# A rule by lag for what stands behind each burst of attention scores, in a two-layer-pair prompt kernel on one core

## The chip, the core and the metric

The kernel runs on one core of one Trainium2 chip. The metric is the device time of one execution in microseconds (us), and the number that counts is the median of several runs. A profile of one execution is shown beside it. In what follows PE is the matrix engine (with its weight loads listed as PEld), ACT the scalar engine, DVE the vector engine, POOL the GpSimd engine, and SP the engine that issues most DMAs.

## What is computed

```python
B, S, D, H = 1, 2048, 576, 32            # Dh = D // H = 18
def _A_ref(x, wq, wk, wv, wo):           # 32 query heads, one shared key and value head
    q = (x @ wq) as (B, H, S, Dh);  k = x @ wk;  v = x @ wv
    scores = einsum("bhqd,bkd->bhqk", q, k) * Dh ** -0.5
    return concat_heads(softmax(scores) @ v) @ wo
def _B_ref(x, wqkv, w_phi, wo):          # linear attention with a learned feature map
    phi(t) = concat(softmax(t @ w_phi), softmax(-t @ w_phi))        # per head
    kv = phi(k).T @ v;  z = phi(k).sum(tokens)
    return (phi(q) @ kv / (phi(q) @ z + 1e-6)) @ wo
x = x + _A_ref(layernorm(x));  x = x + _B_ref(layernorm(x))
x = x + _A_ref(layernorm(x));  x = x + _B_ref(layernorm(x))
```

The two pairs of layers are called layer 0 and layer 1 below.

## The kernel before

Tokens are worked on in 16 tiles of 128. The exact attention of a layer (`attend`) is one long loop over 32 groups: a tile of 128 query tokens with half of the heads makes a group, and a group has 16 key tiles. For one key tile there are two **units** of scores. A unit (`expose`) is two matmuls of 56 rows by 512 columns (line 595) into a score buffer `sc` of two PSUM banks, and one exponential on ACT (line 1101, 128x1024) into a tile `pt` in SBUF. There are three `sc` buffers and `TILES` = 9 tiles `pt`. Two units together feed one **step** of the values (`add_values`, line 875): four matmuls that work on four 32-column strips of the array and add into one PSUM bank. The trace records each of these float32 matmuls twice, so a step is x8 in the profile and x4 in the order of instructions. In one layer the loop has 1012 units and 510 steps.

Two more PSUM banks, named `ps` and `acc`, change roles with every group: one holds the sum of the values, the other is the spare. In the spare bank the loop does the rest of the layer's work in pieces:

- a projection piece, kind `P`: 14 matmuls of 288 columns (line 258), half of a product of a token tile with a weight. Eight make up a period: two for the keys (`wahi`/`walo`), two of the attention's output (`wdhi`/`wdlo`), two for the values (`wbhi`/`wblo`), two for the queries (`wchi`/`wclo`) of the linear attention.
- a piece that updates the state of the linear attention, kind `U`: 32 small matmuls (line 673). One stands at the end of each token tile.
- in layer 0 alone, pieces that fold the feature map into the weights, kind `F` (lines 419 and 429). Twelve of them stand at the start of the loop.

DVE copies each piece out of the spare bank (lines 322, 629, 660, 679), computes the features and, at a group's end, transposes the sum of the values (line 1009). ACT does the exponentials of the features as well (line 636).

The program order on PE and DVE is fixed when the program is written: `in_order()` chains each PE and DVE instruction to the one before. The order is made by a small planner. `at` counts units issued, `done` counts steps issued. A **burst** issues some units of scores, and then something stands in the slot behind them: a piece, some steps, or both. `pace` (0.39 a burst of three units, 0.6 while layer 0 folds) earns a `credit`, and a `P` is placed when the credit has reached 1. `tick()` moves the queues of the other work (`urgent`, `loads`, `slow`) by one stage. In the kernel before, a burst is three units. Where a `P` is due, it alone stands in the slot, and the next slot has values alone (`paused`); other slots have two or three steps, and a `U` comes behind the steps. Only while the planner is told that nothing but values is due (`idle()`) a burst is two units and up to two steps.

Of the kernel before, what the change touches and what calls it, by code (L numbers as in the profile page):

```python
# [19 lines left out]
P = 128  # L20
# [37 lines left out]
def traced(nc):  # L58
    return nc.cur_bb.bb.instructions
# [3 lines left out]
def kernel(ctx, tc, x_in, wq, wk, wv, wo, wqkv, w_phi, wob, out):  # L63
# [518 lines left out]
    def load_shifts(dst, layer, c, g):  # L582
        for j in range(2):
            src = mxds[layer][:, g * HG + j * HG // 2 : g * HG + (j + 1) * HG // 2, c * P : (c + 1) * P]
            to = dst[j * ROWT + KEYS : j * ROWT + STK].bitcast(F32)
            nc.sync.dma_start(to.rearrange("r p (x t) -> r (p x) t", t=P), src)
# [394 lines left out]
    def attend(layer, st, a1o, stream):  # L981
# [7 lines left out]
        def fetch(n):  # L989
            c, g = groups[n]  # L990
            qst[c, g] = a1.tile([P, 2, CW], F32R, name="qst")
            load_queries(qst[c, g], layer, c, g)
            load_shifts(qst[c, g], layer, c, g)

        with ctx1:
# [36 lines left out]
            def values(c, g, t, pt):  # L1032
                if t == 0:
                    homes.reverse()
                    acc[c, g] = bank(*homes[0], [P, CW])
                add_values(acc[c, g], t, [pt[j // 2][:, j % 2, :] for j in range(GH)], t == 0, t == NT - 1)
                if t == NT - 1 and (c, g) == groups[-1]:
                    st["last"] = acc[c, g]
                elif t == NT - 1:
                    finish(c, g)  # L1040
# [8 lines left out]
            def tick():  # L1049
                ticks[0] += 1  # L1050
                for queue in (urgent, loads, slow):
                    begun = len(traced(nc))
                    if queue and next(queue[0], DONE) is DONE:
                        queue.popleft()
                    if queue is loads:
                        for i in traced(nc)[begun:]:
                            if i.engine == mybir.EngineType.SP:
                                tc.add_manual_dep(i, last[PE], SYNC if loads_at[0] is None else NOSYNC, reason="order")
                                loads_at[0] = i.name

            kind, credit, paused = [None], [0.0], [False]

            def peek():
                while kind[0] is None and bulk:
# [20 lines left out]
            def in_order():  # L1085
                for i in traced(nc)[mark[0] :]:
                    if i.engine in PINNED:
                        if i.engine in last:
                            tc.add_manual_dep(i, last[i.engine], NOSYNC, reason="order")
                        last[i.engine] = i.name  # L1090
                mark[0] = len(traced(nc))
# [3 lines left out]
            pts, at, done = {}, [0], [0]  # L1095

            def expose(n, t, hh, pt):
                sc = pss.tile([P, 2, 512], F32, name="sc")
                for j in range(2):
                    score(sc[:, j, :], qst[groups[n]], 2 * hh + j, t)  # L1100
                A.activation(pt, sc, AF.Exp, scale=SCALE)  # L1101
                pts[n, t, hh] = pt

            spots = [*st["head"], *(a1.tile([P, 2, 512], F32, name="pt", bufs=TILES) for _ in range(2 * BURST))]
            acc[groups[0]] = bank(*homes[0], [P, CW])
            at[0] = len(spots)
            done[0] = (at[0] - 2 * BURST) // 2 - 1

            def head_values(t, first, last):
                add_values(acc[groups[0]], t, [pts[0, t, j // 2][:, j % 2, :] for j in range(GH)], first, last)  # L1110

            held = {}

            def head(again):
                for n, (unit, pt) in enumerate(zip(units, spots)):
                    if n >= len(spots) - AHEAD:
                        if not again:
                            held[n] = pss.tile([P, 2, 512], F32, name="sc")
                        for j in range(2):
                            score(held[n][:, j, :], qst[groups[0]], 2 * unit[2] + j, unit[1])  # L1120
                    elif again:
                        expose_by_bank(Spare(), st["q0"], n, pt)
                    elif n >= st["begun"]:
                        expose(*unit, pt)
                    pts[unit] = pt
                    t = n // 2 - BURST
                    if n % 2 and 0 <= t < done[0]:
                        head_values(t, t == 0, False)
# [6 lines left out]
            with tc.If(nc.values_load(safe[0:1, 0:1], min_val=0, max_val=1) == 0):  # L1135
# [5 lines left out]
                for g in range(2):  # L1141
                    load_shifts(st[f"q{g}"], layer, 0, g)
                head_values(BURST - 1, False, True)
                head(True)
# [1 line left out]
                A.activation(spots[n], sc, AF.Exp, scale=SCALE)  # L1146
                st["past"] = traced(nc)[-1].name
            mark[0] = len(traced(nc))
            st["idle"], st["pace"] = lambda: False, 0.0
            view = View(ps=Spare(), a1=a1, loads=loads, slow=slow, finished=finished, ticks=ticks,  # L1150
                        left=lambda: len(units) - at[0])
            bulk.append(stream(view))
# [1 line left out]
            def scores(count):  # L1154
                ready = at[0] // 2
                for n, t, hh in units[at[0] : at[0] + count]:
                    if t == 0 and hh == 0 and 0 < n < len(groups) - 1:
                        fetch(n + 1)
                    expose(n, t, hh, a1.tile([P, 2, 512], F32, name="pt", bufs=TILES))
                    at[0] += 1  # L1160
                in_order()
                return ready

            def sums(until):
                while done[0] < until:
                    n, t, _ = units[2 * done[0]]
                    values(*groups[n], t, [pts.pop((n, t, hh)) for hh in range(2)])
                    done[0] += 1
                    in_order()

            def earn(count):
                credit[0] = min(credit[0] + st["pace"] * count / BURST, 2)

            def burst():
                ready = scores(BURST)
                earn(BURST)
                work = peek()
                tick()
                work = work or peek()
                held = at[0] + BURST - 2 * done[0]  # L1180
                if work == "P" and credit[0] >= 1 and not paused[0] and held <= TILES:
                    fill()
                    credit[0] -= 1
                    paused[0] = True
                else:
                    paused[0] = False
                    count = 3 if credit[0] + st["pace"] >= 1 else 2
                    until = min(ready, max(done[0] + count, -(-(at[0] + BURST - TILES) // 2)))
                    opens = any(t % NT == 0 for t in range(done[0], until))
                    if work == "F" and credit[0] >= 1 and not opens:  # L1190
                        fill()
                        credit[0] -= 1
                        until = min(until, max(done[0] + 1, -(-(at[0] + BURST - TILES) // 2)))
                    sums(until)
                    if work == "U":
                        fill()
                    tick()

            while at[0] < len(units):
                if not st["idle"]():  # L1200
                    burst()
                else:
                    ready = scores(2)
                    sums(min(ready - 1, done[0] + 2))
                    tick()
                    earn(2)
            in_order()
            while done[0] < len(units) // 2:
                sums(done[0] + 1)
# [5 lines left out]
                run(gen)  # L1215

    BURST = 3
    TILES = 9
    DUE = 9
    DUES = {0: 18, 1: 13}  # L1220
# [2 lines left out]
    PACES = ((0.6, 0.39), (0.39, 0.39))  # L1223
# [22 lines left out]
    st = {"late": [], "norms": const.tile([P, NT // PAIR], F32, name="norms"), "wq": weight_tiles("b")}  # L1246
# [8 lines left out]
    def bank(pool, tag, shape):  # L1255
        t = pool.tile([P, CW], F32, name=tag)[: shape[0]]
        if len(shape) == 2:
            return t[:, : shape[1]]
        return t[:, : shape[1] * shape[2]].rearrange("p (a b) -> p a b", b=shape[2])
# [96 lines left out]
    for layer in range(LAYERS):  # L1356
        last = layer == LAYERS - 1
        st.update(start_state(bw), added=set(), loaded=set())
        with tc.tile_pool(name="a1o", bufs=2) as a1o:
# [12 lines left out]
            def stream(v, layer=layer):  # L1372
                ps, loads, slow, finished, ticks = v.ps, v.loads, v.slow, v.finished, v.ticks
                residual = x_in.rearrange("(i p) d -> i p d", p=P) if layer == 0 else xd
                held, spoiled = deque(maxlen=3), set()
                unflipped, st["left"] = deque(), list(range(NT))
                st["closed"], st["pace"] = -1, PACES[layer][0]

                def fetch(src, i):
                    fetch_residual(src, i)  # L1380
# [45 lines left out]
                else:  # L1426
                    loads.append(load_wv())
                    loads.append(load("wk", "a", scratch[1], slice(0, D), padded=True))
                    loads.append(load("wpq", "c", scratch[0], slice(0, D), padded=True))
                st["pace"] = PACES[layer][1]  # L1430
                fetched = xs = None
                weights = False

# [223 lines left out]
```

## Time and profile before

| | |
|---|---|
| median of 3 runs | 2655.14 us (2653.05 to 2656.7) |
| the profiled execution | 2654.06 us, span of its trace 2652.3 us |
| PE busy | 2592.1 us, 98% of the span |
| ACT busy | 2166.2 us, 82% |
| DVE busy | 1248.5 us, 47% |
| DMA queues, share of 16 engines | 31.4% the main one |

A row of the page gives line, engine, operation, output and input tiles with their shapes, the count, the busy time, the mean of one in ns, and behind the second bar how long the engine was idle just before such instructions and what ended that. A row of a timeline gives start, length, engine, line and count, with idle time and its releaser in brackets. Matmuls are pipelined, so the lengths of PE rows overlap; what a group of matmuls costs is the start of the next row less its own start.

Names used below: S3 is a burst's three units of scores (6 matmuls), S2 two units, V1 to V3 one to three steps of values, P and U as above. In the steady part, a period of 64 units and 32 steps (one token tile) holds eight P and one U, and runs from one U to the next.

### The profile page before, as it was taken

The numbers are of one execution on the slowest core, as the hardware profiler recorded it, in microseconds if no ns is written. First come the engines' busy times: TensorE is split into PE (matmuls) and PEld (weight loads), VectorE is DVE, ScalarE is ACT, GpSimd is POOL, SyncE is SP. The second block draws the span as 40 slices with busy tenths as digits, with TensorE's granted clock in tenths as the row PEclk, the third lists the DMA queues.
The fourth block names the chain that finished last, engine by engine and source line by source line (L and its number), as shares of the span: only waits on it lengthen the run. The fifth ranks groups of instructions, "written<-read, shape, count | busy, mean of one in ns | idle before, by whom it ended". The sixth has DMA issues, their size and how long they took to land. (4 is left out here: it accounts for less than half of the span.)

```text
span 2652.3 us, 55525 instructions
## 1 busy us (share of the span) xinstructions
PE 2592.1 (98%) x22002; PEld 1435.2 (54%) x22002; DVE 1248.5 (47%) x2831; ACT 2166.2 (82%) x2578; POOL 66.0 (2%) x106
## 2 busy tenths in 40 slices
PE   7999999999999999999999999999999999999999
PEld 7634454444444444438996344444444444444598
DVE  7334554444444444427774334444444444444265
ACT  5699888999999999993335999999999999999721
POOL 1000000000000000002000000000000000000010
PEclk9999999999999999999999999999999999999999
DMA  6456243222222222225644222222222222222164
GB/s 197 136 143 181 73 136 87 52 65 60 60 60 56 58 60 60 60 53 178 199 130 121 88 60 58 56 59 56 60 60 60 60 60 60 58 51 56 48 200 138
DMA packets 491632, 232.94 MB, mean 88 GB/s; under 512 B 237734, under 2 KB 458214, under 8 KB 491366
## 3 DMA queue, kind: packets, MB, share of 16 engines
q1 hardware_dynamic: 490326, 227.26, 31.4%
q8 instruction: 175, 2.87, 0.5%
q10 hardware_dynamic: 1040, 2.06, 0.3%
q14 instruction: 91, 0.75, 0.1%
HBM read 130.62 MB, written 96.67 MB: 86 GB/s over the span
## 5 line engine op out<-in xcount | busy, mean ns | idle before, releaser
L1101 ACT ACTIVATE pt<-sc 128x1024 f32<-128x1024 f32 x2032 | 1919.5, 1054 | 168.9 <-PE sc L595 142.6
L595 PE MATMUL sc<-qst,kst 56*128 56x512 f32 x3840 | 698.2, 452 | 23.4 <-ACT pt L1101 23.1
L595 PEld LDWEIGHTS sc<-qst,kst 56*128 56x128 f32 x3840 | 318.4, 184 | 563.9 <-ACT pt L1101 517.0
L875 PE MATMUL acc<-pt,vst 128*32 128x512 f32 x4096 | 498.8, 599 | 0.4 <-DVE xc L322 0.2
L875 PE MATMUL ps<-pt,vst 128*32 128x512 f32 x4048 | 482.0, 599 | 0.0
L875 PEld LDWEIGHTS ps<-pt,vst 128*32 128x32 f32 x4048 | 109.6, 109 | 228.6 <-issue 223.1
L875 PEld LDWEIGHTS acc<-pt,vst 128*32 128x32 f32 x4096 | 104.1, 109 | 212.2 <-issue 209.9
L322 DVE TENSOR_TENSOR xc<-xc,acc 128x288 f32<-128x288 f32 x60 | 27.2, 454 | 320.0 <-PE acc L258 320.0
L258 PE MATMUL ps<-wahi,xs 128*128 128x288 f32 x684 | 147.1, 301 | 1.9 <-ACT xs L132 1.9
L258 PE MATMUL ps<-wchi,xs 128*128 128x288 f32 x576 | 127.1, 306 | 0.0
L258 PE MATMUL acc<-wdhi,on 128*128 128x288 f32 x540 | 119.5, 306 | 0.0
L629 DVE COPY featq<-ps 128x288 f32<-128x288 f32 x52 | 23.8, 458 | 198.1 <-PE ps L258 198.1
L258 PEld LDWEIGHTS ps<-wahi,xs 128*128 128x128 f32 x684 | 111.8, 188 | 5.6 <-ACT xs L132 2.6
L258 PE MATMUL ps<-walo,xs 128*128 128x288 f32 x380 | 111.2, 296 | 0.0
L465 PE MATMUL ps<-xsc,wbhi 128*128 128x256 f32 x576 | 107.7, 285 | 0.6 <-ACT xsc L132 0.6
L132 ACT ACTIVATE xs<-ps 128x512 fp32r<-128x512 f32 x36 | 21.4, 595 | 102.6 <-PE ps L308 102.6
L258 PE MATMUL acc<-wahi,xs 128*128 128x288 f32 x468 | 104.0, 307 | 0.4
L258 PEld LDWEIGHTS ps<-wchi,xs 128*128 128x128 f32 x576 | 94.0, 188 | 18.9 <-issue 18.7
L258 PEld LDWEIGHTS acc<-wdhi,on 128*128 128x128 f32 x540 | 88.0, 187 | 21.5 <-issue 20.8
L258 PE MATMUL ps<-wclo,xs 128*128 128x288 f32 x320 | 94.2, 294 | 0.0
L465 PEld LDWEIGHTS ps<-xsc,wbhi 128*128 128x128 f32 x576 | 91.3, 192 | 1.5 <-ACT xsc L132 1.1
L289 POOL TENSOR_TENSOR rstd<-var,neghalf 128x1 f32<-128x1 f32 (+1 forms) x56 | 31.9, 570 | 2343.7 <-DVE var L287 2341.6
(268 smaller groups left out, 3063.5 us busy)
## 6 DMA issues: line engine op xcount, KB each, us to landing
qst<-qd SPq DMA_DIRECT2D x360, 72.0 KB
od<-parts SPq DMA_DIRECT2D x512, 36.0 KB
pht<-phi SPq DMA_DIRECT2D x32, 540.0 KB
qd<-pc SPq DMA_DIRECT2D x64, 256.0 KB
on<-od SPq DMA_DIRECT2D x60, 256.0 KB
phi<-pht SPq DMA_DIRECT2D x104, 144.0 KB
xd<-xc SPq DMA_DIRECT2D x33, 288.0 KB
flipped<-pht SPq DMA_DIRECT2D x112, 72.0 KB
```

The source lines that it names most:

```text
L132: A.activation(dst_hi, src, AF.Copy)
L258: T.matmul(dst, xs[:, slot, :], w[half][:, k, c0 : c0 + HALF], start=(n == 0), stop=(n == last))
L289: G.tensor_tensor(rstd, var, neghalf[:, :n], op=ALU.pow)
L322: V.tensor_add(xr, xr, po)
L465: T.matmul(po, lhs, xsc[:, slot, :], start=(n == 0), stop=(n == LASTP))
L595: T.matmul(sc, kst[head_rows(h), t * P : (t + 1) * P], q[head_rows(h), h // 2, :], start=True, stop=True)
L629: V.tensor_copy(e[:, hs, 0, :], src)
L875: T.matmul(acc[32 * j : 32 * j + 32, :], vst[:, t, :], pts[j], start=first, stop=last)
L1101: A.activation(pt, sc, AF.Exp, scale=SCALE)
```

## The change

The planner is split in three. `fold_burst` is the old burst, for the folding part of layer 0. Elsewhere a burst with a `P` (`project_burst`) is three units and the `P`; it is taken when the `P` has its credit (counted to the end of this burst), the slot before was not a `P`, and the **lag** of the values, `at - 2 * done`, is at most `LAG` = 3 units. All other bursts are `value_burst`: three units right behind a `P` or at an even lag, otherwise two, never above a lag of 9. The number of steps follows from the lag: they bring it down to 3 if a `P` is due soon, to 5 if not, one fewer if a `U` is to follow in the same slot, and at least one where there is no `U`. So where no `P` is due, a burst is two units and one step.

```diff
+            def lag():
+                return at[0] - 2 * done[0]
+            def earned(count):
+                return credit[0] + st["pace"] * count / BURST
-            def burst():
+            def fold_burst():
                 ready = scores(BURST)
...
-                held = at[0] + BURST - 2 * done[0]
-                if work == "P" and credit[0] >= 1 and not paused[0] and held <= TILES:
+                if work == "P" and credit[0] >= 1 and not behind[0] and at[0] + BURST - 2 * done[0] <= TILES:
                     fill()
                     credit[0] -= 1
-                    paused[0] = True
+                    behind[0] = True
                 else:
...
+            def project_burst():
+                scores(BURST)
+                earn(BURST)
+                tick()
+                fill()
+                credit[0] -= 1
+                behind[0] = True
+            def value_burst(idle=False):
+                close = behind[0]
+                count = min(BURST if close or not lag() % 2 else 2, TILES - lag())
+                ready = scores(count)
+                earn(count)
+                work = None if idle else peek()
+                tick()
+                work = None if idle else work or peek()
+                soon = work == "P" and earned(BURST if close else 2 * BURST - 1) >= 1
+                count = (lag() - LAG - (0 if soon else 2)) // 2 - (work == "U")
+                sums(min(ready, done[0] + max(count, 0 if work == "U" else 1)))
+                if work == "U":
+                    fill()
+                behind[0] = False
+                tick()
             while at[0] < len(units):
-                if not st["idle"]():
-                    burst()
+                if st["idle"]():
+                    value_burst(True)
+                elif st["folding"]:
+                    fold_burst()
+                elif kind[0] == "P" and earned(BURST) >= 1 and not behind[0] and lag() <= LAG:
+                    project_burst()
                 else:
-                    ready = scores(2)
-                    sums(min(ready - 1, done[0] + 2))
-                    tick()
-                    earn(2)
+                    value_burst()
...
+    LAG = 3
```

Three places show what this does to the order on PE, and the prediction rests on them. In the rows `sc` is a score buffer (x4 is two units, x6 three), L875 is the values (x4 is one step) and L258 the first rows of a P.

The first place is behind a U in the steady part. Before, the U and what follows up to the keys' first P:

```order
L673 MATMUL ps<-featk,vb_1672 32x36 x32
L595 MATMUL sc<-qst,kst 128x512 x6
L875 MATMUL acc<-pt,vst 32x512 x4
L595 MATMUL sc<-qst,kst 128x512 x4
L875 MATMUL acc<-pt,vst 32x512 x4
L595 MATMUL sc<-qst,kst 128x512 x4
L875 MATMUL acc<-pt,vst 32x512 x4
L595 MATMUL sc<-qst,kst 128x512 x6
L875 MATMUL ps<-pt,vst 32x512 x8
L595 MATMUL sc<-qst,kst 128x512 x6
L258 MATMUL acc<-wahi,xs 128x288
```

The same place on PE now, with the slot of the U in its first row:

```order
L673 MATMUL ps<-featk,vb_1672 32x36 x32
L595 MATMUL sc<-qst,kst 128x512 x4
L875 MATMUL acc<-pt,vst 32x512 x8
L595 MATMUL sc<-qst,kst 128x512 x4
L875 MATMUL acc<-pt,vst 32x512 x4
L595 MATMUL sc<-qst,kst 128x512 x4
L875 MATMUL acc<-pt,vst 32x512 x4
L595 MATMUL sc<-qst,kst 128x512 x4
L875 MATMUL acc<-pt,vst 32x512 x4
L595 MATMUL sc<-qst,kst 128x512 x4
L875 MATMUL ps<-pt,vst 32x512 x8
L595 MATMUL sc<-qst,kst 128x512 x6
```

Between the U and the next P there were ten units and five steps; now there are ten units and seven steps, and the U has one step ahead of it in its slot where it had three.

The second place is on PE between the first and the second P of the values (`wbhi`). Before, behind the first of them:

```order
L595 MATMUL sc<-qst,kst 128x512 x6
L875 MATMUL ps<-pt,vst 32x512 x8
L595 MATMUL sc<-qst,kst 128x512 x6
L875 MATMUL acc<-pt,vst 32x512 x8
L595 MATMUL sc<-qst,kst 128x512 x6
L875 MATMUL acc<-pt,vst 32x512 x8
L595 MATMUL sc<-qst,kst 128x512 x6
L258 MATMUL ps<-wbhi,xs 128x288
```

The same stretch on PE now:

```order
L595 MATMUL sc<-qst,kst 128x512 x6
L875 MATMUL ps<-pt,vst 32x512 x8
L595 MATMUL sc<-qst,kst 128x512 x4
L875 MATMUL acc<-pt,vst 32x512 x8
L595 MATMUL sc<-qst,kst 128x512 x6
L258 MATMUL ps<-wbhi,xs 128x288
```

One of three slots with values went, and one burst lost a unit; the two P that follow have the same shape in front of them now, where before three pairs of S3 P and S3 V3 came in a row.

The third place is the start of the loop on PE in layer 0. Before:

```order
L595 MATMUL sc<-wclo_978,kst 128x512 x6
L875 MATMUL ps<-wahi,vst 32x512 x2
L875 MATMUL ps<-walo,vst 32x512 x2
L875 MATMUL ps<-pt,vst 32x512 x8
L595 MATMUL sc<-wclo_978,kst 128x512 x6
```

And now:

```order
L595 MATMUL sc<-wclo_978,kst 128x512 x2
L875 MATMUL ps<-wahi,vst 32x512 x2
L875 MATMUL ps<-walo,vst 32x512 x2
L875 MATMUL ps<-pt,vst 32x512 x4
L595 MATMUL sc<-wclo_978,kst 128x512 x6
```

The loop began with three units and three steps, and begins with one unit and two steps. The order of DVE's instructions in a steady period is the same as before.

By the order, a steady period had S3 x20, S2 x2, V1 x3, V2 x4, V3 x7, P x8 and U x1 on PE, and has S3 x16, S2 x8, V1 x4, V2 x8, V3 x4, P x8 and U x1. The 12 periods between the first and the last U of layer 1 are all of this shape, before and now. Layer 0 had 187 units up to its first U and has 181; between its first and last U it had 758 units and has 764, of which the first period has 60 (two S2 and two V1 fewer). Both have 67 units behind the last U.

More of the change, by code (lines that the diff above doesn't have):

```diff
@@ L1059, in tick @@
                                 loads_at[0] = i.name
-            kind, credit, paused = [None], [0.0], [False]
+            kind, credit = [None], [0.0]
             def peek():
@@ L1148, in attend @@
             mark[0] = len(traced(nc))
-            st["idle"], st["pace"] = lambda: False, 0.0
+            st["idle"], st["pace"], st["folding"] = lambda: False, 0.0, False
             view = View(ps=Spare(), a1=a1, loads=loads, slow=slow, finished=finished, ticks=ticks,
@@ L1179, in burst @@
                 work = work or peek()
-                held = at[0] + BURST - 2 * done[0]
-                if work == "P" and credit[0] >= 1 and not paused[0] and held <= TILES:
+                if work == "P" and credit[0] >= 1 and not behind[0] and at[0] + BURST - 2 * done[0] <= TILES:
                     fill()
                     credit[0] -= 1
-                    paused[0] = True
+                    behind[0] = True
                 else:
-                    paused[0] = False
+                    behind[0] = False
                     count = 3 if credit[0] + st["pace"] >= 1 else 2
@@ L1197, in burst @@
                     tick()
-            while at[0] < len(units):
-                if not st["idle"]():
-                    burst()
-                else:
-                    ready = scores(2)
-                    sums(min(ready - 1, done[0] + 2))
-                    tick()
-                    earn(2)
+            def project_burst():
[18 more added lines that the diff above has]
+                    fill()
+                behind[0] = False
+                tick()
+            behind = [False]
+            while at[0] < len(units):
+                if st["idle"]():
[4 more added lines that the diff above has]
+                    project_burst()
+                else:
+                    value_burst()
             in_order()
@@ L1376, in stream @@
                 unflipped, st["left"] = deque(), list(range(NT))
-                st["closed"], st["pace"] = -1, PACES[layer][0]
+                st["closed"], st["pace"], st["folding"] = -1, PACES[layer][0], layer == 0
                 def fetch(src, i):
@@ L1429, in stream @@
                     loads.append(load("wpq", "c", scratch[0], slice(0, D), padded=True))
-                st["pace"] = PACES[layer][1]
+                st["pace"], st["folding"] = PACES[layer][1], False
                 fetched = xs = None
```

## The prediction

> **What bounds the kernel.** I read the page's busy table and its costliest groups first:
>
> ```profile
> PE 2592.1 (98%) x22002; PEld 1435.2 (54%) x22002; DVE 1248.5 (47%) x2831; ACT 2166.2 (82%) x2578; POOL 66.0 (2%) x106
> ...
> L1101 ACT ACTIVATE pt<-sc 128x1024 f32<-128x1024 f32 x2032 | 1919.5, 1054 | 168.9 <-PE sc L595 142.6
> L595 PE MATMUL sc<-qst,kst 56*128 56x512 f32 x3840 | 698.2, 452 | 23.4 <-ACT pt L1101 23.1
> ```
>
> ACT waits 142.6 us for scores in all, and PE looks full. It is not quite: lengths of PE rows overlap, so I read starts. Next I cut the loop into periods, by the timeline's rows of U (first and last of each layer), with the sums over one period by stretches:
>
> ```profile
> 317.69 0.75 PE L673 MATMUL acc<-featk,vb 128*32 128x36 f32 x64
> ...
> 1131.83 0.75 PE L673 MATMUL ps<-featk,vb 128*32 128x36 f32 x64
> ...
> 1617.07 0.75 PE L673 MATMUL ps<-featk,vb 128*32 128x36 f32 x64
> ...
> 2437.25 0.75 PE L673 MATMUL ps<-featk,vb 128*32 128x36 f32 x64
> ...
> 926.57:994.89 68.32, 67.70 (x564) 33.28 (x560) 30.34 (x61) 62.92 (x69) 0.54 (x1) 1.00 0.24 58
> ```
>
> So 12 periods take 820.18 us in layer 1 (68.35 each) and 814.14 us in layer 0: 62% of the span. The columns behind the length are PE, PEld, DVE and ACT busy. The third view is PE's timeline at a period's start, which shows who waits:
>
> ```profile
> 926.57 0.75 PE L673 MATMUL ps<-featk,vb 128*32 128x36 f32 x64
> 927.26 0.97 PE L595 MATMUL sc<-qst,kst 56*128 56x512 f32 x6
> 928.15 1.06 PE L875 MATMUL acc<-pt,vst 128*32 128x512 f32 x8
> 929.15 0.50 PE L595 MATMUL sc<-qst,kst 56*128 56x512 f32 x2
> 929.85 0.49 PE L595 MATMUL sc<-qst,kst 56*128 56x512 f32 x2 [0.20 <-ACT pt L1101]
> 930.27 1.07 PE L875 MATMUL acc<-pt,vst 128*32 128x512 f32 x8
> 931.27 0.91 PE L595 MATMUL sc<-qst,kst 56*128 56x512 f32 x4
> 932.11 1.06 PE L875 MATMUL acc<-pt,vst 128*32 128x512 f32 x8
> 933.11 0.91 PE L595 MATMUL sc<-qst,kst 56*128 56x512 f32 x4
> 934.43 0.49 PE L595 MATMUL sc<-qst,kst 56*128 56x512 f32 x2 [0.42 <-ACT pt L1101]
> 934.86 1.92 PE L875 MATMUL ps<-pt,vst 128*32 128x512 f32 x16
> 936.71 0.97 PE L595 MATMUL sc<-qst,kst 56*128 56x512 f32 x6
> 937.61 0.40 PE L258 MATMUL acc<-wahi,xs 128*128 128x288 f32 x1
> ...
> 939.67 1.06 PE L595 MATMUL sc<-qst,kst 56*128 56x512 f32 x6
> 940.65 2.78 PE L875 MATMUL ps<-pt,vst 128*32 128x512 f32 x24
> 943.37 0.96 PE L595 MATMUL sc<-qst,kst 56*128 56x512 f32 x6
> ```
>
> Start to start: S3 0.90 (936.71), P 2.06, S3 behind a P 0.98, V3 2.72, V2 1.85, U 0.69. The S3 at 933.11 took 1.75, so it waited 0.85 for ACT to free score buffers. Two bursts that did not wait give S2 0.66 and V1 1.00:
>
> ```profile
> 588.43 0.73 PE L595 MATMUL sc<-qst,kst 56*128 56x512 f32 x4
> 589.09 1.07 PE L875 MATMUL acc<-pt,vst 128*32 128x512 f32 x8
> 590.09 0.73 PE L595 MATMUL sc<-qst,kst 56*128 56x512 f32 x4
> ```
>
> At these prices the old period (S3 12x0.90 + 8x0.98, S2 2x0.66, V1 3x1.00, V2 4x1.85, V3 7x2.72, P 8x2.06, U 0.69) is 66.57 us. It lasts 68.32, so PE waits 1.75 in it; 1.48 of that lies in the stretch 927.26 to 936.71 (9.45 us for 7.97 of work). ACT's pace:
>
> ```profile
> 927.86 9.27 ACT L1101 ACTIVATE pt<-sc 128x1024 f32<-128x1024 f32 x10 [0.86 <-PE sc L595]
> ...
> 943.00 0.70 ACT L636 ACTIVATE featk<-featk 128x576 f32<-128x576 f32 x1
> ...
> 1160.23 5.81 ACT L1101 ACTIVATE pt<-sc 128x1024 f32<-128x1024 f32 x6 [0.86 <-PE sc L595]
> ```
>
> Ten exponentials in 9.27, the last lasting 1.05: one per 0.91 us. A period's 64 units and four of line 636 need 61.0, so over the period PE is the bound, and wherever it waits for ACT that time is lost: behind a P ACT starves, behind a U PE runs into full score buffers.
>
> **The change, part by part.** *Work.* Matmuls and exponentials are the same. A period gets two more groups of scores and two more of values. A group of values costs 0.14 beside its steps (1.00 against 0.86 more per step), one of scores 0.18 beside its units (0.90 less 0.66 is 0.24 a unit): 0.64 more. The new period (S3 8x0.90 + 8x0.98, S2 8x0.66, V1 4x1.00, V2 8x1.85, V3 4x2.72, P, U) comes to 67.17.
>
> [...]
>
> *Waits behind the U.* Put time 0 at the S3 behind the last P. Its exponentials start at 0.60 (927.26 to 927.86) and end by 3.5; line 636 takes 0.70; the ten units behind the U then end from 5.1 on every 0.91. PE reaches the five S2 at 2.67, 5.18, 6.84, 8.50, 10.16 and the next S3 at 12.67. A unit needs the exponential three units earlier. The second units of the middle three S2 want ends of 5.1, 6.9 and 8.7 and come 0.1 to 0.4 later; the fifth wants 10.5 and waits 0.1, and the S3's third unit about 0.1. So 0.2 remains of 1.75: the extra two steps fill the time in which PE waited. In the three stretches S3 P S3 V2 S2 V2 (8.30 us) ACT needs 8x0.91 + 0.70 = 8.0, and PE does not wait. New period 67.37.
>
> *The sum.* Layer 1's periods: 820.18 - 12x67.37 = 11.7. Layer 0's: 814.14 - 11x67.37 - 64.05 (first period: two S2, two V1 fewer) = 9.0. The 54 units before a layer's first U, which in layer 1 began here:
>
> ```profile
> 1558.91 0.97 PE L595 MATMUL sc<-qst,kst 56*128 56x512 f32 x6
> ```
>
> took 58.16 to the U; the new order is 4x6.66 (S3 P S3 V3) + 3x8.30 + 4.94 = 56.48: 1.7 in each layer, 3.4. In three places (two tails, layer 1's first pair of P) the second P of a pair gets S3 V2 S2 V1 behind it for S3 V3; ACT's 0.86 of starving (1160.23) is covered there: 2.6. At the loop's start ACT starved for the V3:
>
> ```profile
> 128.39 2.86 ACT L1101 ACTIVATE pt<-sc 128x1024 f32<-128x1024 f32 x3 [3.01 <-PE sc L595]
> ```
>
> Now a V2 and 0.60 of latency stand behind one unit: 1.85 + 0.60 - 0.91 = 1.5; 1.5 saved in each layer, 3.0. Layer 0 up to its first U has six units less (they are in its periods above): two less at the start (2x0.91), three more and a V1 among the folding (0.90 + 1.00), seven less behind it at 0.92 (931.27 to 933.11 is 1.84 for two): 6.3. In all 36.0. The profiled execution took 2654.06, so 2618; the median is 1.1 above it: 2619 us, 1.4% faster.
>
> *Costed at nothing.* DMA issues are the same, at most a slot earlier or later; queries are fetched a group (over 30 us) ahead. The U comes 2.0 us behind the last P's end where it came 3.7, and needs that P's copy (0.46) off the bank. The attention's output P stand as far behind the group's end as before. DVE's order is unchanged, but one cover shrinks: the transposition of a group's sum must clear the bank before the second P of the values. DVE at that place:
>
> ```profile
> 966.39 0.46 DVE L660 COPY vb<-acc 128x288 f32<-128x288 f32 x1 [6.19 <-PE acc L258]
> ...
> 970.65 0.71 DVE L1009 STREAM_TRANSPOSE turned<-ps 128x512 f32<-128x512 f32 x1
> ```
>
> It is done 5.0 us behind the first P; PE now comes back in 0.98 + 1.85 + 0.66 + 1.85 + 0.90 = 6.2. That leaves 1.2.
>
> *Bounds.* New waits of nothing take 5 off, and the V1 before the U may be 0.1 cheaper: 2611. Half the old waits (0.9 a period) add 17: 2636.
>
> **The rivals.** First, S2 always waits for ACT. In the row at 931.27 an S2 between V1 takes 0.84. My 36 us are spread over 190 S2 in the periods, 0.19 each, so at 0.85 all is lost: about 2654, no change. Against it: such bursts settle at 0.84 only when PE is ahead by all three buffers for long; here a P comes after five. Second, the other sign by the same wait, if the lag rule starves and blocks in turn as at 929.15 (1.12 for an S2): 190x0.46 is 87 more than forecast, some 2706. It needs ACT late by a unit at each S2; line 636 with 0.70 alone does not do that. Third, DVE: if it is 2.4 us later at line 1009, PE waits 1.2 a period, 29 in all: 2648. At 47% busy little speaks for it. Fourth, the folding: its pieces come two units earlier, and DMA is tight there, as one wait of DVE in the list of waits shows:
>
> ```profile
> DVE wdhi L134 <- DMA wstage<-in_A_wo_dram: 30.4, 5, 13.2
> ```
>
> If a fold piece on PE waits 8 us, of the 13.2 that DVE waited at most, the result is 2627. That the change moves nothing is excluded: the order shows it.
>
> **How the numbers follow.** The forecast has 0.80, the folding's wait 0.05, DVE's 0.06, S2 at 0.84 0.05, S2 at 1.12 0.04. The time is the forecast's, 2619. The range 2610 to 2640 takes in both bounds and the folding, and leaves out 0.15. About 0.2% (5 us) is what the measurement can tell from no change: faster 0.91, same 0.05, slower 0.04.
>
> **What would show it.** Right: U to U near 67.4 in steady periods, S2 at 0.66 with the first waits in the fifth behind a U; S3 P S3 V2 S2 V2 in 8.3; ACT's wait for scores at line 1101 down by some 35 from 142.6; PE's wait for ACT at line 595 (23.1) mostly gone. Wrong: S2 rows at 0.84 or more behind each P, a PE wait for DVE at a P's first row, or a fold piece that waits for a DMA.

## The result, and the profile after

The changed kernel takes 2625.69 us (median of 4 runs, 2624.53 to 2628.34), the kernel before 2654.10 in the same session (2652.38 to 2656.7). The ratio is 0.9894 with a 95% interval of 0.9876 to 0.9911: 28 us, 1.1%, faster. The forecast was 2619, 36 us faster, with a range of 2610 to 2640. The profiled execution's span is 2624.6 for 2652.3.

The busy table and the two groups that were read first, on the page of the changed kernel:

```profile
PE 2585.7 (99%) x22002; PEld 1428.7 (54%) x22002; DVE 1252.3 (48%) x2831; ACT 2163.5 (82%) x2578; POOL 66.0 (3%) x106
...
L1101 ACT ACTIVATE pt<-sc 128x1024 f32<-128x1024 f32 x2032 | 1923.4, 1062 | 146.8 <-PE sc L595 120.1
L595 PE MATMUL sc<-qst,kst 56*128 56x512 f32 x3840 | 687.3, 449 | 1.7 <-ACT pt L1101 1.4
```

PE's recorded wait for ACT at the scores went from 23.1 to 1.4 us; ACT's wait for scores from 142.6 to 120.1, 22.5 less where the forecast had some 35. Next the first and last U of each layer's 12 periods, and one steady period by the view of stretches (length, PE, PEld, DVE and ACT busy, granted clock):

```profile
312.90 0.75 PE L673 MATMUL ps<-featk,vb 128*32 128x36 f32 x64
...
1119.65 0.75 PE L673 MATMUL ps<-featk,vb 128*32 128x36 f32 x64
...
1600.45 0.75 PE L673 MATMUL ps<-featk,vb 128*32 128x36 f32 x64
...
2408.89 0.75 PE L673 MATMUL ps<-featk,vb 128*32 128x36 f32 x64
...
917.28:984.64 67.36, 67.36 (x564) 33.04 (x560) 30.46 (x62) 62.82 (x69) 0.54 (x1) 1.00 0.24 59
```

Layer 1's periods take 808.44 us (67.37 each; forecast 67.37), layer 0's 806.75. The timeline of PE behind the U at 984.64 shows how; read it from start to start:

```profile
984.64 0.75 PE L673 MATMUL ps<-featk,vb 128*32 128x36 f32 x64
985.32 0.73 PE L595 MATMUL sc<-qst,kst 56*128 56x512 f32 x4
985.99 1.92 PE L875 MATMUL acc<-pt,vst 128*32 128x512 f32 x16
987.84 0.73 PE L595 MATMUL sc<-qst,kst 56*128 56x512 f32 x4
988.51 1.07 PE L875 MATMUL acc<-pt,vst 128*32 128x512 f32 x8
989.50 0.73 PE L595 MATMUL sc<-qst,kst 56*128 56x512 f32 x4
990.17 1.07 PE L875 MATMUL acc<-pt,vst 128*32 128x512 f32 x8
991.16 0.86 PE L595 MATMUL sc<-qst,kst 56*128 56x512 f32 x4
991.95 1.06 PE L875 MATMUL acc<-pt,vst 128*32 128x512 f32 x8
992.95 0.91 PE L595 MATMUL sc<-qst,kst 56*128 56x512 f32 x4
993.78 1.92 PE L875 MATMUL ps<-pt,vst 128*32 128x512 f32 x16
```

The first three S2 take 0.67, 0.67 and 0.67: no wait. The fourth takes 0.79, the fifth 0.83, so PE waits 0.3 there, where the old stretch from U to the next P held 1.48 of waits. ACT, on its timeline behind a U one period earlier, has no idle time left in front of the ten exponentials, where it had 0.86:

```profile
918.83 0.70 ACT L636 ACTIVATE featq<-featq 128x576 f32<-128x576 f32 x1
919.40 9.28 ACT L1101 ACTIVATE pt<-sc 128x1024 f32<-128x1024 f32 x10
```

### The profile page after: what moved, and what is told of

The parts are those of the page before. It is cut to its first block, busy times and chain, and to the rows that moved or that the text cites. A ratio compares the mean times of both kernels' runs of the same rounds, so it can differ in the third digit from the quotient of the medians.

```text
span 2624.6 us, 55489 instructions
## 1 busy us (share of the span) xinstructions
PE 2585.7 (99%) x22002; PEld 1428.7 (54%) x22002; DVE 1252.3 (48%) x2831; ACT 2163.5 (82%) x2578; POOL 66.0 (3%) x106
## 5 line engine op out<-in xcount | busy, mean ns | idle before, releaser
L1101 ACT ACTIVATE pt<-sc 128x1024 f32<-128x1024 f32 x2032 | 1923.4, 1062 | 146.8 <-PE sc L595 120.1
L595 PE MATMUL sc<-qst,kst 56*128 56x512 f32 x3840 | 687.3, 449 | 1.7 <-ACT pt L1101 1.4
L875 PE MATMUL acc<-pt,vst 128*32 128x512 f32 x4096 | 510.7, 600 | 0.2 <-DVE vb L660 0.2
L875 PE MATMUL ps<-pt,vst 128*32 128x512 f32 x4048 | 483.4, 600 | 0.0
L875 PEld LDWEIGHTS ps<-pt,vst 128*32 128x32 f32 x4048 | 108.9, 109 | 225.8 <-issue 225.0
L875 PEld LDWEIGHTS acc<-pt,vst 128*32 128x32 f32 x4096 | 98.5, 108 | 201.0 <-issue 189.1
L258 PE MATMUL ps<-wahi,xs 128*128 128x288 f32 x684 | 147.0, 301 | 1.9 <-ACT xs L132 1.9
L258 PE MATMUL ps<-wchi,xs 128*128 128x288 f32 x576 | 127.4, 306 | 0.0
L258 PE MATMUL acc<-wdhi,on 128*128 128x288 f32 x531 | 117.4, 306 | 0.0
L258 PEld LDWEIGHTS ps<-wahi,xs 128*128 128x128 f32 x684 | 111.8, 188 | 5.6 <-ACT xs L132 2.6
L258 PE MATMUL ps<-walo,xs 128*128 128x288 f32 x380 | 111.2, 295 | 0.0
L258 PE MATMUL acc<-wahi,xs 128*128 128x288 f32 x468 | 103.8, 307 | 1.3 <-DVE turned L1009 1.3
L258 PEld LDWEIGHTS ps<-wchi,xs 128*128 128x128 f32 x576 | 94.0, 188 | 16.1 <-issue 15.7
L258 PEld LDWEIGHTS acc<-wdhi,on 128*128 128x128 f32 x531 | 86.5, 187 | 21.2 <-issue 21.2
L629 DVE COPY featk<-acc 128x288 f32<-128x288 f32 x52 | 23.8, 457 | 153.2 <-PE acc L258 153.2
L258 PE MATMUL ps<-wclo,xs 128*128 128x288 f32 x320 | 94.2, 294 | 0.0
```

What stands on the lines that cost most here:

```text
L258: T.matmul(dst, xs[:, slot, :], w[half][:, k, c0 : c0 + HALF], start=(n == 0), stop=(n == last))
L595: T.matmul(sc, kst[head_rows(h), t * P : (t + 1) * P], q[head_rows(h), h // 2, :], start=True, stop=True)
L629: V.tensor_copy(e[:, hs, 0, :], src)
L875: T.matmul(acc[32 * j : 32 * j + 32, :], vst[:, t, :], pts[j], start=first, stop=last)
```

## The experiments

The theory: PE waits for ACT around the U and the P, and the change fills those waits by putting two steps off behind the U and by spreading the steps evenly, at a price of four more boundaries between groups. Rivals: the order of the matmuls itself is cheaper on PE; or only one of the two moves matters.

**ACT's load halved, on both kernels.** The edit is the same in the kernel before and in the changed one. It leaves out half of the loop's exponentials and keeps every matmul and its place, so that PE runs each kernel's order with almost no ACT to wait for (its recorded wait at line 595 is 1.2 and 0.0 us):

```diff
-                A.activation(pt, sc, AF.Exp, scale=SCALE)
+                if short:
+                    A.activation(pt[:, 0, :], sc[:, 0, :], AF.Exp, scale=SCALE)
+                    cut.add((n, t, hh))
+                else:
+                    A.activation(pt, sc, AF.Exp, scale=SCALE)
...
-                add_values(acc[c, g], t, [pt[j // 2][:, j % 2, :] for j in range(GH)], t == 0, t == NT - 1)
+                add_values(acc[c, g], t, [pt[j // 2][:, 0 if short[j // 2] else j % 2, :] for j in range(GH)], t == 0, t == NT - 1)
```

> The kernel before, with ACT's load halved: in the loop the exponential is taken of the first 512 columns of each unit alone, and the values use that half twice (half of the loop's exponentials are left out; every matmul, its order and its size stay). Theory (PE's waits for ACT are what the change removes, and its four more boundaries of groups a period cost 0.64): without waits for ACT a steady period falls from 68.3 to about 66.2 (65.7 to 66.6, the prices of its rows without waits), and PE's wait for ACT at line 595 falls from 23 to under 2 us; in all 2550 to 2600 us, since the stretches that ACT paces fall too. Rival (the gain comes from the order of matmuls on PE itself): the period stays over 67.5.

> The changed kernel with the same cut (the exponential of the loop's units on their first half alone, used twice by the values; order of matmuls as in the changed kernel). Theory: with no wait for ACT to remove, the change only leaves its four more boundaries a period: periods 0.5 to 0.7 longer than in the halved kernel before (about 66.8), so this one is about 14 us slower in the 24 periods, where the change in full was 28 us faster. Rival (the order of matmuls itself is cheaper): periods about 1 us shorter than in the halved kernel before, some 25 us faster. [...]

Measured: 2557.52 us with the old order, 2574.77 with the new one (ratios to the kernel before 0.9629, interval 0.9613 to 0.9645, and 0.9695, 0.9679 to 0.9711). The first and last U of layer 1 in each, on PE's timeline, first of the halved kernel before:

```profile
1563.15 0.75 PE L673 MATMUL ps<-featk,vb 128*32 128x36 f32 x64
...
2351.31 0.75 PE L673 MATMUL ps<-featk,vb 128*32 128x36 f32 x64
```

and of the halved changed kernel:

```profile
1568.80 0.75 PE L673 MATMUL ps<-featk,vb 128*32 128x36 f32 x64
...
2364.36 0.75 PE L673 MATMUL ps<-featk,vb 128*32 128x36 f32 x64
```

That is 65.68 and 66.30 a period: without ACT's load the change is a loss of 0.62 a period and of 17 us in all. The rival of a cheaper order falls. A table of four splits the gain:

| period, us | full exponentials | half | lost to ACT |
|---|---|---|---|
| order before | 68.32 | 65.68 | 2.64 |
| order now | 67.37 | 66.30 | 1.07 |
| now less before | -0.95 | +0.62 | -1.57 |

The 0.62 is the forecast's 0.64 for four more boundaries. The weight loads last 185 ns for scores and 109 for values, on the mean of the halved changed kernel's page:

```profile
L595 PEld LDWEIGHTS sc<-qst,kst 56*128 56x128 f32 x3840 | 304.1, 185 | 471.2 <-ACT pt L1104 317.8
L875 PEld LDWEIGHTS ps<-pt,vst 128*32 128x32 f32 x4048 | 108.7, 109 | 250.3 <-issue 249.5
```

Two of each are 0.59, so these runs do not show that a boundary costs more than its load.

**The U's slot.** Two edits of one line of the changed kernel. The first (u_closed) closes the lag in front of the U again, three steps there as before the change; the second (u_steps) puts off one step fewer:

```diff
-                count = (lag() - LAG - (0 if soon else 2)) // 2 - (work == "U")
+                count = (lag() - LAG - (0 if soon or work == "U" else 2)) // 2
```

```diff
-                count = (lag() - LAG - (0 if soon else 2)) // 2 - (work == "U")
+                count = (lag() - LAG - (0 if soon else 2)) // 2
```

> The changed kernel, but in front of the state's update U the slot closes the lag as before the change: S3 V3 U, then S2 V1 five times, where the changed kernel has S3 V1 U and more steps behind it. Number of groups in a period as in the changed kernel. Theory (the two steps moved behind the U are what keeps ACT fed and gives it time to free buffers): the first S2 comes 4.39 behind the S3, ACT is free at 4.1 and gets its scores at 5.0, so it starves 0.9, and PE waits 0.6 to 0.9 for buffers in the five S2 and the S3 behind them: period 67.9 to 68.2 for 67.4, in all 2637 to 2645 us. Rival (the bursts of two units in the idle slots are what matters, the U's own slot does not): period stays at 67.4 and the time at 2626.

> The changed kernel with one step more in front of the U (its rule for fewer steps there removed): S3 V2 U, S2 V1 four times, S2 V2. Groups of a period as in the changed kernel. Theory: the first S2 comes 3.52 behind the S3 and its first exponential could start at 4.1, when ACT is done with line 636, so ACT just does not starve and nothing is lost: period 67.3 to 67.6, the tail behind a layer's last U up to 0.9 shorter since ACT has a smaller backlog there; in all 2622 to 2630 us. Rival (both steps have to be put off): 0.4 to 0.9 a period more, 2635 to 2647 us.

u_closed took 2644.74 (ratio to before 0.9967, interval 0.9954 to 0.9979), u_steps 2627.81 (0.9898, 0.9881 to 0.9914). The last U's of layer 1 lie 68.15 apart in u_closed, 67.38 in u_steps. In u_closed ACT starves behind the V3 and the U, and PE then waits; first a row of ACT's timeline, then PE's in the same period:

```profile
990.74 10.19 ACT L1101 ACTIVATE pt<-sc 128x1024 f32<-128x1024 f32 x11 [0.75 <-PE sc L595]
```

```profile
998.74 0.91 PE L595 MATMUL sc<-qst,kst 56*128 56x512 f32 x4
1000.06 0.50 PE L595 MATMUL sc<-qst,kst 56*128 56x512 f32 x2 [0.41 <-ACT pt L1101]
```

The two rows are one S3 that starts at 998.74; its third unit waits 0.41 for a buffer. So the U's own slot is worth 0.78 a period here, and of the steps put off behind it one is enough: the second changes nothing (67.38 against 67.37).

**One part alone, in the kernel before.** One line gives the old rule two steps in front of the U and leaves the rest as it was (before_u1):

```diff
                     count = 3 if credit[0] + st["pace"] >= 1 else 2
+                    count = 1 if work == "U" else count
```

(The buffers' bound adds one step to that one.) Two edits of the changed kernel try the bursts: no_spread closes the lag everywhere but at the U, so that V3 S2 V1 stands where V2 S2 V2 was; threes_busy keeps the steps behind the U and takes bursts of three outside idle slots.

```diff
-                count = (lag() - LAG - (0 if soon else 2)) // 2 - (work == "U")
+                count = (lag() - LAG) // 2 - (work == "U")
```

```diff
-                count = min(BURST if close or not lag() % 2 else 2, TILES - lag())
+                count = min(2 if idle and not close and lag() % 2 else BURST, TILES - lag())
```

> The kernel before with one line more: in front of the U, two steps of values instead of three (the third goes behind the U; all other bursts as before the change, so no more groups than before). Worked out by laying one period's order end to end with the rows' prices (S 0.18 + 0.24 a unit, V 0.14 + 0.86 a step, P 2.06, an exponential 0.91 that starts 0.36 behind its unit, three score buffers, a buffer free 0.18 behind its exponential), which gives 68.25, 67.31, 68.08 and 67.32 for before, changed, u_closed and u_steps where the traces show 68.32, 67.37, 68.15 and 67.38. Theory (the steps put off behind the U are the whole gain): period 67.4 to 67.6, in all 2630 to 2637 us. Rival (the two-step, two-unit bursts behind each P carry half of it or more): period 67.9 or longer, 2643 us or more.

> The changed kernel whose slot always closes the lag to three units, but for the step put off in front of the U: behind the second P-pairs stands S3 P S3 V3 S2 V1 where the changed kernel has S3 P S3 V2 S2 V2; at the U S3 V2 U S2 V2. Same number of groups a period. By the same adding-up: the V3 starves ACT for 1.1 in each of three such stretches and PE then waits in the S3 around the next P: period 68.7 to 69.1, 1.4 to 1.7 more than the changed kernel's 67.37, in all 2660 to 2668 us: slower than the kernel before. Rival (only the U's slot matters; ACT has 0.3 of slack in each stretch, which takes it up): period 67.4 to 67.6, 2626 to 2631 us.

> The changed kernel with bursts of three units again outside the idle slots, but with its steps put off behind the U: S3 V2 S3 V2 S3 V2 for S3 V2 S2 V2 in the last pairs, and S2 V2 S2 V1 S3 V2 S3 V2 behind the U: two groups of scores and two of values fewer a period (0.64 less to do). By the same adding-up the S3 between V2 wait for ACT what the boundaries save: period 67.4 to 67.6, in all 2622 to 2632 us, the changed kernel's time. Rival (the number of groups decides): period 66.7, 2608 to 2612 us, a better kernel than the changed one.

| kernel | us | ratio to before, interval | steady period, us |
|---|---|---|---|
| before_u1 | 2633.15 | 0.9921 (0.9904 to 0.9937) | 67.49 |
| no_spread | 2672.57 | 1.0069 (1.0052 to 1.0086) | 69.09 |
| threes_busy | 2643.75 | 0.9958 (0.9944 to 0.9972) | 68.15 (layer 0), 67.83 (layer 1) |

before_u1 lands where the theory put it: one step moved past the U gives 0.83 of the 0.95 a period and 21 of the 28 us, with no more boundaries than before. no_spread shows the other half: the same number of groups, a step put off at the U, and yet slower than before. ACT's timeline of no_spread in that stretch:

```profile
1044.53 4.69 ACT L1101 ACTIVATE pt<-sc 128x1024 f32<-128x1024 f32 x5 [0.80 <-PE sc L595]
1049.61 2.86 ACT L1101 ACTIVATE pt<-sc 128x1024 f32<-128x1024 f32 x3 [0.39 <-PE sc L595]
```

ACT starves 0.80 and 0.39 for eight exponentials, and then PE stands at the buffers: from start to start an S3 takes some 1.36 for 0.90 in each of the three stretches, and 1.75 ahead of the keys' first P, where the fifth S2 behind the U has one step behind it for two. Its page has 28.3 us of PE waiting for ACT at line 595 and 178.9 of ACT waiting for PE, both above the kernel before's 23.1 and 142.6. Its time lies above the expected 2660 to 2668, in part since two units more stand in its tails (81.8 behind the last U of each layer to the next, for 79.9). threes_busy missed my sum: 67.83 in layer 1 for the expected 67.4 to 67.6, and 0.3 more in layer 0; why stays open. Its PE timeline shows one S3 of such a run:

```profile
2162.13 1.92 PE L875 MATMUL ps<-pt,vst 128*32 128x512 f32 x16
2163.98 1.27 PE L595 MATMUL sc<-qst,kst 56*128 56x512 f32 x6
```

The S3 at 2163.98 lasts 1.27 for 0.97 in an S3 without waits. The page of threes_busy has 10.5 us of such recorded waits where the changed kernel's has 1.4. So fewer boundaries did not pay: the rival by which their number decides, with 66.7 a period, falls. No kernel tried beats the changed one by more than these runs can tell.

**The loop's start.** The forecast gave the new first burst (S2 V2 for S3 V3) 1.5 us in each layer. An edit puts the old first burst back, and it was run twice, the second time beside the changed kernel once more (after2):

```diff
-                if st["idle"]():
+                if at[0] == len(spots):
+                    scores(BURST)
+                    earn(BURST)
+                    peek()
+                    tick()
+                    sums(done[0] + 3)
+                    tick()
+                elif st["idle"]():
```

> The changed kernel whose loops begin with the old first burst (S3 V3 for S2 V2): tests the term of the loop's start. Theory of the forecast: ACT starves 1.5 longer in each layer, all of it lost: 3 us slower than the changed kernel (2629 us), at the first pieces of folding and in layer 1's first 54 units. Rival (PE runs at half clock there in the changed kernel too, so that ACT is not what sets the pace): within 1 us of the changed kernel, 2625 to 2627 us.

> The changed kernel once more, for a second trace of its loop starts beside old_start2: in its first trace layer 0's loop took 201.2 us from its first scores to the first U, in old_start's 197.6, where the forecast had 197.2. If the 4 us belong to the order behind the new first burst, this trace shows 201 to 203 again; if they come from where the half-clock windows fall in one run, it can show anything from 197 to 203. In all 2624 to 2629 us.

> The changed kernel with the old first burst, once more. Theory one (the new first burst makes layer 0's start longer, the reverse of the forecast's term): 197 to 199 us from the first scores to the first U again, and the time 2 to 4 us below after2. Theory two (the start is set by the half-clock windows of a run): within 201 us or more, or after2 comes to 198, and the times are within 2 us of each other.

| kernel | us | ratio to before, interval | layer 0: first scores to first U | layer 1: the same |
|---|---|---|---|---|
| changed | 2625.69 | 0.9894 (0.9876 to 0.9911) | 201.20 | 180.13 |
| after2 | 2627.38 | 0.9897 (0.9879 to 0.9915) | 199.09 | 180.59 |
| old_start | 2626.48 | 0.9895 (0.9879 to 0.9912) | 197.56 | 180.00 |
| old_start2 | 2625.42 | 0.9891 (0.9874 to 0.9909) | 196.10 | 182.57 |

By the times the new first burst is worth nothing. In layer 0 it even stands 3.3 us behind on the mean of two traces, though the first U comes two units earlier in old_start's order. Measured to layer 0's last U, where both have done the same work, it is 3.0 behind (1007.95 and 1005.92 for 1004.63 and 1003.25). In layer 1 it is 0.9 ahead. Neither theory of the second pair is shown, since the same kernel differs from itself by up to 2.6 here. What it differs by is the clock. The view of stretches from layer 1's first scores to the end of its first V3 (length, then PE, PEld, DVE, ACT and POOL busy, then the granted clock) in old_start and in old_start2, which are the same program:

```profile
1419.55:1431.11 11.56, 10.18 (x59) 3.04 (x59) 0.10 (x1) 10.24 (x11) 0.00 (x0) 0.85 0.27 80
```

```profile
1414.95:1429.09 14.14, 13.06 (x58) 3.42 (x58) 1.14 (x3) 10.24 (x11) 0.00 (x0) 0.66 0.32 97
```

In the first the V3 took 2.71 us, in the second 4.38.

## Why the prediction was right, and where its sum was off

*Right: the mechanism and the period.* The steady period is 67.37 as forecast, layer 1's periods gave 11.74 for 11.7, and the 54 units before its first U took 56.37 (1544.08 to 1600.45) for 56.48. The halved kernels show both of its parts, boundaries at 0.62 (forecast 0.64) and waits. S2 between V's take 0.67, with the first waits in the fourth and fifth behind the U (forecast: the fifth), and the three stretches S3 P S3 V2 S2 V2 last 8.3 each. S2 at 0.84 in every place (rival one) and starving in turn (rival two) did not happen; no_spread shows that the other sign was near: a few steps placed otherwise cost 1.7 a period.

One price was read wrongly without harm. I took 0.98 for an S3 behind a P as its work. In the halved changed kernel, on PE's timeline, it takes 0.89:

```profile
1016.68 0.96 PE L595 MATMUL sc<-qst,kst 56*128 56x512 f32 x6
1017.57 1.92 PE L875 MATMUL acc<-pt,vst 128*32 128x512 f32 x16
```

So some 0.09 of it is a wait for ACT, in seven of the eight such places of a period. It stands in the old and in the new order, and the difference kept its size. Together these waits are 0.65 of the 1.07 that the changed order still loses to ACT. Both halved periods came some 0.5 below what was expected of them (66.2 and 66.8) in the main for this.

*Off: 8.3 us of the 36 are missing.* By the profiled executions the gain is 27.7 in the span. Four terms of the sum carry the difference.

The tails: -0.86 each was forecast, and +0.60 came in layer 0. PE's timeline has the last U of a period and the next U, before:

```profile
1131.83 0.75 PE L673 MATMUL ps<-featk,vb 128*32 128x36 f32 x64
...
1211.16 0.77 PE L673 MATMUL ps<-featk,vb 128*32 128x36 f32 x64
```

and after:

```profile
1119.65 0.75 PE L673 MATMUL ps<-featk,vb 128*32 128x36 f32 x64
...
1199.58 0.77 PE L673 MATMUL ps<-featk,vb 128*32 128x36 f32 x64
```

79.33 became 79.93. Two steps failed here. One is a reading of ACT's rows: the 0.86 of starving at 1160.23 stands behind the V3 of the pair's first P, where the order did not change, and ACT's timeline of the changed kernel has it still:

```profile
1148.81 5.82 ACT L1101 ACTIVATE pt<-sc 128x1024 f32<-128x1024 f32 x6 [0.86 <-PE sc L595]
```

Behind the second P, where S3 V3 became S3 V2 S2 V1, ACT had line 298 to do in the kernel before and did not starve: there was nothing to cover. (In layer 1's first pair of P, without line 298, the 0.82 there did go.) The other step is bookkeeping: I booked 1.7 a layer as gained in the 54 units up to the first U, where two steps fewer are done by then, and forgot that the last U hands those two steps (2x0.86 = 1.72) to the tail. Between two U's the debt is passed on; behind the last one it is paid. The halved kernels show it bare: their tails last 73.54 and 75.42, 1.88 more; and u_steps, which hands on one step fewer, has 79.18. With full exponentials much of the tail goes at ACT's pace (S2 V1 in 1.83 where PE's work is 1.66), and the debt shows as a later start of ACT behind the U: 2.03 us behind it for 1.28, by the rows of ACT before and after.

```profile
1133.11 20.27 ACT L1101 ACTIVATE pt<-sc 128x1024 f32<-128x1024 f32 x22 [0.86 <-PE sc L595]
```

```profile
1121.68 20.28 ACT L1101 ACTIVATE pt<-sc 128x1024 f32<-128x1024 f32 x22
```

Of these 0.75, 0.60 are left at the next U. Layer 1's tail has +0.68. Measured on to the next loop's start and to the core's end (+0.84 and +0.66 for -0.86 each) this is 3.2 of the 8.3.

Layer 0 up to its first U: 9.5 were forecast between the first scores and the U, and of the old 206.70 us 5.5 went in this trace and 7.6 in after2; the loop also began 0.7 later. That is 4.7 of the 8.3. The rows of the fold's pieces (lines 419 and 429; the first at 157.67 and the last at 232.71 before, at 158.09 and 237.01 now) split it.

Up to the first piece 3.3 were forecast, two units and the loop's start, and 0.3 went. Here falls the loop's start. This stretch lasts 45.1 to 47.0 us in the four traces with the old first burst and full exponentials and 44.3 to 46.4 in the six with the new one: 1.2 less on the mean, where two units alone are 1.8. The term of 1.5 took ACT's starving there for the limit, but PE runs at half clock in part of it (a granted 0.50 from 121.90 to 125.30 in the changed kernel), which is the likely cause and was not tested apart. On the changed kernel's PE timeline the V2 of layer 0's start lasts 3.57 (121.87 to 125.44) where a V2 costs 1.85:

```profile
121.87 1.07 PE L875 MATMUL ps<-wahi,vst 128*32 128x512 f32 x2
...
123.58 1.94 PE L875 MATMUL ps<-pt,vst 128*32 128x512 f32 x8
125.44 1.07 PE L595 MATMUL sc<-wclo,kst 56*128 56x512 f32 x6
```

This trace has a second such stretch some 24 us into the loop, which after2, 1.9 faster up to the first piece, has not (the view of stretches, the granted clock behind POOL; first after, then after2):

```profile
135.70:139.70 4.00, 3.77 (x18) 0.88 (x18) 1.91 (x3) 2.93 (x4) 0.00 (x0) 0.57 0.95 163
```

```profile
136.00:140.00 4.00, 4.00 (x32) 1.18 (x32) 1.91 (x3) 3.82 (x5) 0.00 (x0) 1.00 0.92 173
```

Among the pieces three units and a V1 more were forecast at 1.90, their work on PE, and 3.9 came (3.6 in after2). Two bursts of scores hold most of the difference. One S3 takes 2.05 (201.83 to 203.88) for 0.90, since two of its units wait for ACT, and another takes 1.67, since the P behind it waits for DVE, which none did there before:

```profile
202.53 0.50 PE L595 MATMUL sc<-qst,kst 56*128 56x512 f32 x2 [0.20 <-ACT pt L1101]
203.45 0.49 PE L595 MATMUL sc<-qst,kst 56*128 56x512 f32 x2 [0.42 <-ACT pt L1101]
...
220.16 0.40 PE L258 MATMUL ps<-wdhi,on 128*128 128x288 f32 x1 [0.70 <-DVE turned L1009]
```

Behind the last piece 9.1 went for the forecast's 8.1. No fold piece was seen waiting 8 us, as the fourth rival had it.

Layer 0's first period: 65.62 for 64.05, 1.6 of the 8.3. There PE waits for DVE at line 1009, as in the third rival:

```profile
322.58 0.40 PE L258 MATMUL acc<-wahi,xs 128*128 128x288 f32 x1 [1.33 <-DVE turned L1009]
```

DVE is not late by its own work. Its rows of line 1009 in this period and in the next end 9.6 us behind their U (at 312.90 and 378.53) alike:

```profile
321.85 0.68 DVE L1009 STREAM_TRANSPOSE turned<-acc 128x512 f32<-128x512 f32 x1
...
387.48 0.67 DVE L1009 STREAM_TRANSPOSE turned<-acc 128x512 f32<-128x512 f32 x1
```

PE is early: this period has two S2 and two V1 fewer ahead of the P, 3.3 us, and in the next one the P stands 11.7 behind the U. The forecast booked these 3.3 as gained and did not ask what they had covered. In the steady periods the cover of 1.2 held, as forecast.

Layer 1 up to its first U went the other way: 5.3 less than the old 185.42 for the 4.1 of the forecast (lead-in, one pair, start), inside what two traces of one program differ by there.

The forecast of ACT's wait, 35 less, failed with the sum: 24 periods of 0.95 are 22.8, and two traces of the changed kernel show 22.5 and 25.7 less.

## What to carry to other kernels

Where two engines pass buffers to each other and the slower one is not the bound on average, look for the few slots where a long item of the bound (here V3 and U in a row, 2.60 and 0.68 us with no scores) outlasts what is queued for the other: moving one step past such an item, one line of code, gave three quarters of this gain. Halving the second engine's load in both versions, with the order kept, splits such a change into what it costs and what it saves. In a sum by stretches, a step put off out of one stretch has to be booked in the one where it is paid, and work taken out of a stretch may have covered another engine's.

## What the runs showed of the hardware

The start of each loop runs at a granted clock that differs from run to run: the mean from layer 1's first scores to the end of its first V3 was 0.85 and 0.66 in two runs of the same program, and the V3 there took 2.71 or 4.38 us; in layer 0 the 4 us from some 136 on were at 0.57 and 1.00 in two traces of the changed kernel. The view of stretches at layer 0's start in the changed kernel, with the same columns:

```profile
115.10:118.50 3.40, 1.09 (x9) 0.34 (x10) 0.65 (x5) 1.95 (x3) 0.00 (x0) 0.95 0.07 17
118.50:121.90 3.40, 2.86 (x18) 1.11 (x11) 0.00 (x0) 3.16 (x4) 0.00 (x0) 0.55 0.14 38
121.90:125.30 3.40, 3.40 (x17) 0.56 (x16) 0.25 (x1) 1.52 (x2) 0.00 (x0) 0.50 0.66 193
```

A stretch with PE busy for 1.09 of 3.40 us, at a clock of 0.95, is followed by two at 0.55 and 0.50, in which PE is busy all but 0.54 us. What sets the clock there no run shows.

So a term of 1 or 2 us at such a place cannot be told by one trace. And ACT's slack over a period does not keep PE from waiting for it: an S3 behind a P lost some 0.09 at seven of eight places a period, with ACT busy 62.82 of 67.36 us.
